# A 96-row gather, a fold split over two engines, a shuffle in pieces and earlier loads in the start of a Fourier and feed-forward kernel

## The chip, the cores and the metric

The kernel runs on one core of a Trainium2 chip. The metric is the device time of one execution in microseconds (us). Every execution quoted here counts as fast: none took over 1.5% more than the fastest of the same kernel. Engines are named as the profile names them: PE is TensorE's matmuls and PEld its weight loads, DVE is VectorE, ACT is ScalarE, POOL is GpSimd, and SP is SyncE, which here only issues transfers. A `q` after an engine's name (SPq, POOLq) means its sequencer.

## The reference, cut to what matters

The input is 8 batches of 3008 rows by 256 columns. The kernel takes the real part of a two-dimensional Fourier transform of each batch and sends all rows through a gated feed-forward block.

```python
def _attn_ref(x):                       # x: (8, 3008, 256)
    X = np.fft.fft(x, axis=1)
    X = np.fft.fft(X, axis=2)
    return X.real.astype(np.float32)

def _moe_ref(x, w_gate, w_val, w_out):  # x: (24064, 256), d_ff = 1536
    gate = np.maximum(x @ w_gate, 0.0)
    val = x @ w_val
    return (gate * val @ w_out).astype(np.float32)
```

## The kernel before

The kernel writes the 3008 rows as 94 times 32. For one batch the work is a chain:

1. `load_x`: half of x comes by two plain transfers (`xl`), the other half, in reversed order of blocks, by a gather (`xh`): a transfer that fetches one row per index, with one index for each partition (row of the on-chip memory).
2. `fold`: sums and differences of mirrored rows and columns, elementwise, into `eo`.
3. `stage1`: 17 row groups of `eo` times small Fourier tables on TensorE, into `t1`.
4. `shuffle`: `t1` is written to memory (`Td`) and read back in another order (`t4`).
5. `rotate` and `stage2`: the second half of the transform along the rows, into `pq`.
6. The main loop: 288 steps (`plus`, `minus`, `out_piece`), 36 per batch. The transform along the columns is multiplied into the weights beforehand (the weight products `psw`, into `wc`, `ws`, `wm`).

Batch 0 does 1 to 5 before the loop. Batch b+1 does 3 to 5 inside the loop of batch b, at step numbers set in the table `extra`. The parts that matter here, with cuts marked by `...`:

```python
NA, NB = 94, 32
def load_x(b):
    xl = xp.tile([NA, J, D], F32, tag="xl")
    xh = xp.tile([NA, NB // 2, D], F32, tag="xh")
    for p0, n in ((0, 80), (80, 14)):
        nc.sync.dma_start(out=xl[p0:p0 + n], in_=...)
    nc.gpsimd.indirect_dma_start(out=xh[:]..., in_=...,
                                 in_offset=bass.IndirectOffsetOnAxis(ap=ix[:, b:b + 1], axis=0))
...
def shuffle(b):
    nc.sync.dma_start(out=Td[b], in_=t1t.pop(b)[:]...)
    t4 = tp.tile([128, NKA, D], BF16, tag="t4")
    nc.sync.dma_start(out=t4[:], in_=view(Td[b], 0, [[D, 128], [128 * D, NKA], [1, D]]))
...
ix = const.tile([NA, B], I32, tag="ix")
nc.gpsimd.iota(ix[:], pattern=[[2 * NA, B]], base=2 * NA - 1, channel_multiplier=-2)
load_x(0)
...                                   # weight loads, w_out, all tables on VectorE
fold(0, nc.vector)
for c in range(8):
    stage1(0, c, "act" if c % 2 else "dve")
shuffle(0)
load_x(1)
fold(1, nc.gpsimd)
for i in range(2):                    # weight products
    for n in range(DF // 512):
        ...
rotate(0)
...                                   # stage2(0), then the main loop with
for b in range(B):
    t0 = b * NBLK * NF
    # load_x(b+2) at t0+10, fold(b+2) on GpSimd at t0+11,
    # stage1(b+1) at t0+1..8, shuffle at t0+9, rotate at t0+16, stage2 at t0+18+3i
```

Of the kernel before, what the change touches and what calls it, by code (L numbers as in the profile page):

```python
# [10 lines left out]
F32 = mybir.dt.float32  # L11
# [20 lines left out]
def sin_of(nc, sp, out, t, n, shape):  # L32

    q = sp.tile(shape, F32, tag="q")
    nc.vector.tensor_scalar(q[:], t, scalar1=1.0 / n, scalar2=RND, op0=ALU.mult, op1=ALU.add)
    nc.vector.tensor_scalar(q[:], q[:], scalar1=-RND, scalar2=float(n), op0=ALU.add, op1=ALU.mult)
    nc.vector.tensor_tensor(q[:], t, q[:], op=ALU.subtract)
    nc.scalar.activation(out, q[:], ACTF.Sin, scale=2.0 * math.pi / n * (1.0 - 2e-7))
# [3 lines left out]
def kernel(ctx: ExitStack, tc, x, w_gate, w_val, w_out, out):  # L42
# [9 lines left out]
    NKA = 12  # L52
# [16 lines left out]
    def load_x(b):  # L69
        xl = xp.tile([NA, J, D], F32, tag="xl")  # L70
        xh = xp.tile([NA, NB // 2, D], F32, tag="xh")
        for p0, n in ((0, 80), (80, 14)):
            nc.sync.dma_start(out=xl[p0:p0 + n],  # L73
                              in_=view(x, b * S * D + p0 * NB * D, [[NB * D, n], [1, J * D]]))
# [4 lines left out]
        xt[b] = (xl, xh)  # L79

    eot = {}

    def fold(b, eng):
        xl, xh = xt.pop(b)
        xc = xp.tile([NA, J - 2, D], F32, tag="xc")
        eo = tp.tile([NA, J, D], BF16, tag="eo")
        n = J - 2
        rev = free(xh[:], n * D, [-D, n], [1, D])
        eng.tensor_tensor(xc[:], xl[:, 1:J - 1, :], rev, op=ALU.subtract)  # L89
        eng.tensor_tensor(xl[:, 1:J - 1, :], xl[:, 1:J - 1, :], rev, op=ALU.add)  # L90
        eng.tensor_tensor(eo[:, :, 1:H], xl[:, :, 1:H], free(xl[:], D - 1, [D, J], [-1, H - 1]), op=ALU.add)
        eng.tensor_tensor(eo[:, 1:J - 1, H + 1:D], xc[:, :, 1:H],
                          free(xc[:], D - 1, [D, n], [-1, H - 1]), op=ALU.subtract)
        eng.tensor_tensor(free(eo[:], H + 1, [(J - 1) * D, 2], [1, H - 1]),
                          free(xl[:], 1, [(J - 1) * D, 2], [1, H - 1]),
                          free(xl[:], D - 1, [(J - 1) * D, 2], [-1, H - 1]), op=ALU.subtract)
        eng.tensor_copy(free(eo[:], 0, [D, J], [H, 2]), free(xl[:], 0, [D, J], [H, 2]))  # L97
        eot[b] = eo
# [3 lines left out]
    def stage1(b, c, evac):  # L102
        if c == 0:
            t1t[b] = tp.tile([96, 16, D], BF16, tag="t1", bufs=1, name="t1")
        t1, eo = t1t[b], eot[b]
# [20 lines left out]
    def shuffle(b):  # L126
        nc.sync.dma_start(out=Td[b], in_=t1t.pop(b)[:].rearrange("p j d -> p (j d)"))
        t4 = tp.tile([128, NKA, D], BF16, tag="t4")
        nc.sync.dma_start(out=t4[:], in_=view(Td[b], 0, [[D, 128], [128 * D, NKA], [1, D]]))
        t4t[b] = t4  # L130
# [23 lines left out]
    ix = const.tile([NA, B], I32, tag="ix")  # L154
    nc.gpsimd.iota(ix[:], pattern=[[2 * NA, B]], base=2 * NA - 1, channel_multiplier=-2)
    load_x(0)
# [11 lines left out]
    with tc.tile_pool(name="st", bufs=1, space=SB) as st, \  # L168
# [8 lines left out]
        nc.gpsimd.dma_start(out=wo[:], in_=view(w_out, 0, [[D, 128], [128 * D, NF], [1, D]]))  # L177
# [12 lines left out]
        for off in (S // 4, S // 2):  # L190
# [3 lines left out]
            sin_of(nc, sp, tb[:], t2[:], S, [NA, J, 48])  # L194
# [6 lines left out]
        nc.vector.memset(w1[:, 0, :], 0.0)  # L201

# [14 lines left out]
        nc.vector.tensor_scalar(z[:], jj[:], scalar1=0.0, scalar2=None, op0=ALU.is_equal)  # L217
        zs = sp.tile([128, 1], F32, tag="zs")
        nc.vector.tensor_tensor(zs[:], z[:], sl[:], op=ALU.mult)
        mul = sp.tile([128, 1], F32, tag="mul")  # L220
        nc.vector.tensor_scalar(mul[:], zs[:], scalar1=16.0, scalar2=None, op0=ALU.mult)
        nc.vector.tensor_tensor(mul[:], mul[:], jj[:], op=ALU.add)
        offs = []

        for cs, (o0, d1) in enumerate(((8.0, -8.0), (16.0, -8.0))):
            o = sp.tile([128, 1], F32, tag=f"off{cs}")
            nc.vector.tensor_scalar(o[:], sl[:], scalar1=d1, scalar2=o0 - 8.0, op0=ALU.mult, op1=ALU.add)
# [212 lines left out]
```

## Time and profile before

| Reading | Value |
|---|---|
| time, median of the runs beside the change | 821.86 us |
| span of the profiled run | 820.7 us |
| first gather issued, and landed | 1.79 us, 51.9 us |
| main loop starts | 108.6 us |
| TensorE waits inside the loop | 24.4 us and 9.5 us, both in batch 0 |
| TensorE busy from 200 to 280 us | 79.88 of 80 us |

From 200 us on TensorE is full. What can be won lies before. The view of waits lists who waited for whom, for how many us in total, how often, and the longest. These are TensorE's four longest in the kernel before:

```profile
PE ps_240 L115 <- DVE eo L97: 65.3, 1, 65.3
PE ps_434 L115 <- POOL eo L97: 24.4, 1, 24.4
PE psr L135 <- DMA t_276<-Td: 12.7, 1, 12.7
PE psr L135 <- DMA t_590<-Td: 9.5, 1, 9.5
```

The first is batch 0's fold on VectorE, the second batch 1's fold on GpSimd inside the loop. The last two are the reads of the two batches' shuffles. The timeline gives, for each instruction, its start, its duration, engine, source line, operation and shapes, and in brackets how long the engine was idle before it and what ended that:

```profile
51.93 4.15 DVE L89 TENSOR_TENSOR xc<-xl,xh 94x3840 f32<-94x3840 f32 x1 [27.54 <-DMA xh<-in_x_dram,ix]
...
104.95 0.19 PE L135 MATMUL psr<-t_276,rot 128*128 128x12 bf16 x1 [12.69 <-DMA t_276<-Td]
...
108.58 0.63 PE L325 MATMUL G<-pq,wc_84 128*128 128x512 bf16 x1
...
110.22 8.27 POOL L89 TENSOR_TENSOR xc<-xl,xh 94x3840 f32<-94x3840 f32 x1 [46.09 <-DMA xl<-in_x_dram]
```

VectorE stood idle for 27.54 us until the gather had landed. The view of windows shows why the gather took so long. After the length of the window it gives the busy us (and the instructions) of PE, PEld, DVE, ACT and POOL, then TensorE's granted clock. Its last two columns are the mean busy share of the 16 DMA engines, and the GB/s that they moved:

```profile
30.00:35.00 5.00, 0.00 (x0) 0.00 (x0) 0.00 (x0) 0.00 (x0) 0.00 (x0) 1.00 0.12 52
...
40.00:45.00 5.00, 0.00 (x0) 0.00 (x0) 0.00 (x0) 0.00 (x0) 0.00 (x0) 1.00 0.13 53
...
200.00:280.00 80.00, 79.88 (x533) 50.91 (x532) 55.29 (x84) 47.79 (x83) 26.60 (x8) 1.00 0.36 99
```

Between 30 and 45 us no engine runs an instruction, and the gather, together with what is left of other loads, keeps a share of 0.12 to 0.13 busy: two engines' worth of 16. The summary of this gather's eight executions says that this is not only so at the start:

```profile
DMA to landing us min/median/max: 34.8/37.5/50.1
```

### The profile page before, as it was taken

To read this page: it belongs to the slowest core of one execution; us is meant where nothing else is said; L and a number is where in the kernel's file an instruction comes from. 1 tells how busy PE (TensorE), PEld (TensorE's weight loads), DVE (VectorE), ACT (ScalarE), POOL (GpSimd) and SP (SyncE) were. 2 spreads that over 40 slices of the span, in tenths; PEclk is the share of its full clock that TensorE was granted. 3 is DMA by queue.
4 is the path that set the end of the run, shared out by engine and by line. 5 is a ranking of instruction groups with operands and counts; after the bars stand their busy time and mean duration, and the time that the engine had idled before them with its cause. 6 is when DMAs were issued, how large, how long until landed. Compare 5 with 4: busy or idle time off the path is not lost.

```text
span 820.7 us, 12157 instructions
## 1 busy us (share of the span) xinstructions
PE 696.3 (85%) x4432; PEld 433.2 (53%) x4432; DVE 491.5 (60%) x767; ACT 406.4 (50%) x699; POOL 203.8 (25%) x66
## 2 busy tenths in 40 slices
PE   0007433859999999999999999999999999999997
PEld 0004211336666666666666666666666666666655
DVE  6143121636776676667666766676666666666662
ACT  1002211525565656565656565656565655655552
POOL 2001067009300930094009400850093000000000
PEclk9999865979999999999999999999999999999999
DMA  9302510262137213621271226212711141111112
GB/s 242 77 28 79 130 23 10 88 135 51 53 99 184 50 54 98 168 67 48 88 193 47 61 89 177 64 50 81 192 55 43 26 127 27 51 29 48 35 43 76
DMA packets 31852, 67.37 MB, mean 82 GB/s; under 512 B 9040, under 2 KB 22864, under 8 KB 29520
## 3 DMA queue, kind: packets, MB, share of 16 engines
q1 hardware_dynamic: 24096, 53.48, 25.8%
q0 software_dynamic: 7696, 13.13, 4.9%
q8 instruction: 34, 0.56, 0.3%
q14 instruction: 26, 0.21, 0.1%
HBM read 36.42 MB, written 30.93 MB: 82 GB/s over the span
## 4 chain that ended last, share of the span: by engine, by line
PE 74%; DVE 7%; DMA 6%; POOL 4%; another core or an unknown queue 3%; SPq 2%; ACT 2%; issue 1%; POOLq 0%; DVEq 0%
PE po L359 28%; PE V L336 9%; PE G L325 7%; PE G L326 7%; PE V L326 7%; PE V L325 7%; PE G L336 7%; DVE h L329 2%; DMA t_590<-Td 2%; SPq L73 2%; DMA xl<-in_x_dram 2%; ACT gs L339 1%; DMA Td<-t_433 1%; DMA Td<-t_239 1%
## 5 line engine op out<-in xcount | busy, mean ns | idle before, releaser
L341 DVE TENSOR_TENSOR h<-gs,V 128x512 bf16<-128x512 f32 x288 | 198.1, 688 | 199.9 <-ACT gs L339 147.4
L359 PE MATMUL po<-wo,h 128*128 128x256 bf16 x2304 | 297.8, 273 | 0.0
L339 ACT ACTIVATE gs<-G 128x512 f32<-128x512 f32 x288 | 172.2, 598 | 241.4 <-PE G L336 241.4
L359 PEld LDWEIGHTS <-h 128*128 128x128 bf16 x2304 | 223.4, 98 | 74.3 <-issue 10.5
L329 DVE TENSOR_TENSOR h<-gs,V 128x512 bf16<-128x512 f32 x288 | 197.8, 687 | 10.9 <-ACT gs L328 5.7
L328 ACT ACTIVATE gs<-G 128x512 f32<-128x512 f32 x288 | 172.3, 598 | 30.2 <-PE G L326 13.6
L89 POOL TENSOR_TENSOR xc<-xl,xh 94x3840 f32<-94x3840 f32 x7 | 58.2, 8314 | 362.8 <-DMA xl<-in_x_dram 362.8
L336 PE MATMUL V<-pq,wm_89 128*128 128x512 bf16 x288 | 109.0, 379 | 5.0 <-DVE h L329 3.6
L336 PE MATMUL G<-pq,wm_88 128*128 128x512 bf16 x288 | 109.8, 381 | 1.0 <-ACT gs L328 0.8
L326 PE MATMUL V<-pq,ws_87 128*128 128x512 bf16 x288 | 109.8, 381 | 0.0
L325 PE MATMUL V<-pq,wc_85 128*128 128x512 bf16 x288 | 109.7, 381 | 0.0
L326 PE MATMUL G<-pq,ws_86 128*128 128x512 bf16 x288 | 109.6, 381 | 0.0
L325 PE MATMUL G<-pq,wc_84 128*128 128x512 bf16 x288 | 109.5, 380 | 0.0
L90 POOL TENSOR_TENSOR xl<-xl,xh 94x3840 f32<-94x3840 f32 x7 | 58.2, 8316 | 0.6
L115 PE MATMUL ps_240<-eo,wz 94*96 94x129 bf16 (+1 forms) x4 | 0.6, 303 | 65.3 <-DVE eo L97 65.3
L325 PEld LDWEIGHTS <-wc_84 128*128 128x128 bf16 x288 | 27.8, 97 | 52.8 <-issue 42.0
L115 PEld LDWEIGHTS <-wz 94*96 94x96 bf16 x32 | 3.2, 136 | 91.2 <-issue 77.3
L365 ACT COPY os<-po 128x512 f32<-128x512 f32 x48 | 28.1, 585 | 43.8 <-PE po L359 43.8
L326 PEld LDWEIGHTS <-ws_87 128*128 128x128 bf16 x288 | 28.2, 98 | 34.7 <-issue 0.8
L325 PEld LDWEIGHTS <-wc_85 128*128 128x128 bf16 x288 | 28.0, 97 | 34.8 <-issue 0.8
L326 PEld LDWEIGHTS <-ws_86 128*128 128x128 bf16 x288 | 27.8, 97 | 34.5 <-issue 0.6
L363 DVE COPY os<-po 128x512 f32<-128x512 f32 x48 | 33.2, 692 | 8.4 <-PE po L359 8.4
(341 smaller groups left out, 381.7 us busy)
## 6 DMA issues: line engine op xcount, KB each, us to landing
out_dram<-os SPq DMA_DIRECT2D x176, 128.0 KB, 2.6
xl<-in_x_dram SPq DMA_DIRECT2D x8, 1360.0 KB, 11.8
xl<-in_x_dram SPq DMA_DIRECT2D x8, 238.0 KB
wst_100<-in_moe_w_gate_dram SPq DMA_DIRECT2D x2, 768.0 KB, 23.9
wst_103<-in_moe_w_val_dram SPq DMA_DIRECT2D x2, 768.0 KB, 34.5
out_dram<-os SPq DMA_DIRECT2D x16, 96.0 KB, 1.8
wo<-in_moe_w_out_dram POOLq DMA_DIRECT2D x1, 768.0 KB, 52.3
Td<-t_239 SPq DMA_DIRECT2D x1, 768.0 KB, 9.3
```

The lines of the kernel that those rows point to most:

```text
L89: eng.tensor_tensor(xc[:], xl[:, 1:J - 1, :], rev, op=ALU.subtract)
L90: eng.tensor_tensor(xl[:, 1:J - 1, :], xl[:, 1:J - 1, :], rev, op=ALU.add)
L325: nc.tensor.matmul(acc[:], lhsT=wc[i][:, fs], rhs=pq[:, 0, :], start=True, stop=False)
L326: nc.tensor.matmul(acc[:], lhsT=ws[i][:, fs], rhs=pq[:, 1, :], start=False, stop=True)
L328: nc.scalar.activation(gs[:], G[:], ACTF.Relu)
L329: nc.vector.tensor_tensor(h[:, 0, :], gs[:], V[:], op=ALU.mult)
L336: nc.tensor.matmul(acc[:], lhsT=wm[i][:, fs], rhs=pq[:, 1, :], start=False, stop=True, skip_group_check=True)
L339: nc.scalar.activation(gs[:], G[:], ACTF.Relu)
L341: nc.vector.tensor_tensor(free(h[:], 512 + NB - 1, [NB, 16], [-1, NB]), gs[:].rearrange("p (a k) -> p a k", k=NB), V[:].rearrange("p (a k) ...
L359: nc.tensor.matmul(po[:, s % 2, :], lhsT=ht[b, blk, ff][:, sg, g * 128:(g + 1) * 128], rhs=wo[:, ff, :], start=(ff == 0), stop=(ff == NF - 1))
L363: nc.vector.tensor_copy(os_[:, s - 1:s + 1, :], po[:])
L365: nc.scalar.copy(os_[:, s - 1:s + 1, :], po[:])
```

## The change

The intent is to shorten the start. Its parts are:

- the gather uses 96 rows instead of 94; the two extra indices are clamped to 0 and their rows are not used;
- batch 0's fold is split by rows: rows 1 to 11 and the ends on VectorE, rows 12 to 15 on GpSimd;
- most of the small tables move from VectorE to GpSimd, which computes them before its rows;
- batch 0's shuffle is written in four pieces and read in three;
- batch 1's loads, and w_out, are issued before the shuffle's read instead of after it (and w_out instead of at the very start);
- in the loop of batch 0, batch 1's stages come at later steps; those of the other batches shift by a few;
- smaller things: stage 1 takes row group 0 last and is emptied mostly by ScalarE, and the groups of weight products come in another order.

The diff, cut to its core:

```diff
-        xh = xp.tile([NA, NB // 2, D], F32, tag="xh")
+        xh = xp.tile([96, NB // 2, D], F32, tag="xh")
...
-    ix = const.tile([NA, B], I32, tag="ix")
+    ix = const.tile([96, B], I32, tag="ix")
     nc.gpsimd.iota(ix[:], pattern=[[2 * NA, B]], base=2 * NA - 1, channel_multiplier=-2)
-    load_x(0)
+    nc.gpsimd.tensor_scalar(ix[:], ix[:], scalar1=0, scalar2=None, op0=ALU.max)
+    load_x(0, nc.sync)
...
-        nc.gpsimd.dma_start(out=wo[:], in_=view(w_out, 0, ...))
...
+        pl = nc.gpsimd          # the small tables now on pl, their sines still on ScalarE
...
-        fold(0, nc.vector)
-        for c in range(8):
-            stage1(0, c, "act" if c % 2 else "dve")
-        shuffle(0)
-        load_x(1)
-        fold(1, nc.gpsimd)
+        fold(0, nc.vector, 2, 8)
+        fold(0, nc.vector, 8, 12)
+        fold(0, nc.gpsimd, 12, 16)
+        fold_ends(0, nc.vector)
+        fold(0, nc.vector, 1, 2)
+        for k, c in enumerate((1, 2, 3, 4, 5, 6, 7, 0)):
+            stage1(0, c, "dve" if k in (5, 7) else "act")
+        for k in (2, 4, 6, 0):
+            shuffle_out(0, k, k + 2)
+        load_x(1, nc.scalar)
+        nc.gpsimd.dma_start(out=wo[:], in_=view(w_out, 0, ...))
+        for blk in range(NBLK):
+            shuffle_in(0, 4 * blk, 4 * blk + 4)
+        fold_all(1)
...
+        tl, t1, tr, t2, d2 = (17, 16, 28, 29, 1) if b == 0 else (10, 4, 19, 20, 2)
+        # load_x(b+2) at tl, stage1(b+1) from t1, shuffle at t1+8, rotate at tr, stage2 from t2 every d2
```

More of the change, by code (lines that the diff above doesn't have):

```diff
@@ L29, in free, with sin_of @@
     return bass.AP(ap.tensor, ap.offset + offset, [part] + [list(d) for d in dims])
-def sin_of(nc, sp, out, t, n, shape):
+def sin_of(nc, eng, sp, out, t, n, shape):
     q = sp.tile(shape, F32, tag="q")
-    nc.vector.tensor_scalar(q[:], t, scalar1=1.0 / n, scalar2=RND, op0=ALU.mult, op1=ALU.add)
-    nc.vector.tensor_scalar(q[:], q[:], scalar1=-RND, scalar2=float(n), op0=ALU.add, op1=ALU.mult)
-    nc.vector.tensor_tensor(q[:], t, q[:], op=ALU.subtract)
+    eng.tensor_scalar(q[:], t, scalar1=1.0 / n, scalar2=RND, op0=ALU.mult, op1=ALU.add)
+    eng.tensor_scalar(q[:], q[:], scalar1=-RND, scalar2=float(n), op0=ALU.add, op1=ALU.mult)
+    eng.tensor_tensor(q[:], t, q[:], op=ALU.subtract)
     nc.scalar.activation(out, q[:], ACTF.Sin, scale=2.0 * math.pi / n * (1.0 - 2e-7))
@@ L67, with load_x @@
     xt = {}
-    def load_x(b):
+    def load_x(b, q):
         xl = xp.tile([NA, J, D], F32, tag="xl")
-        xh = xp.tile([NA, NB // 2, D], F32, tag="xh")
+        xh = xp.tile([96, NB // 2, D], F32, tag="xh")
         for p0, n in ((0, 80), (80, 14)):
-            nc.sync.dma_start(out=xl[p0:p0 + n],
-                              in_=view(x, b * S * D + p0 * NB * D, [[NB * D, n], [1, J * D]]))
+            q.dma_start(out=xl[p0:p0 + n],
+                        in_=view(x, b * S * D + p0 * NB * D, [[NB * D, n], [1, J * D]]))
         nc.gpsimd.indirect_dma_start(out=xh[:].rearrange("p j d -> p (j d)"), out_offset=None,
@@ L78, in load_x @@
                                      in_offset=bass.IndirectOffsetOnAxis(ap=ix[:, b:b + 1], axis=0))
-        xt[b] = (xl, xh)
-    eot = {}
-    def fold(b, eng):
-        xl, xh = xt.pop(b)
-        xc = xp.tile([NA, J - 2, D], F32, tag="xc")
-        eo = tp.tile([NA, J, D], BF16, tag="eo")
-        n = J - 2
-        rev = free(xh[:], n * D, [-D, n], [1, D])
-        eng.tensor_tensor(xc[:], xl[:, 1:J - 1, :], rev, op=ALU.subtract)
-        eng.tensor_tensor(xl[:, 1:J - 1, :], xl[:, 1:J - 1, :], rev, op=ALU.add)
-        eng.tensor_tensor(eo[:, :, 1:H], xl[:, :, 1:H], free(xl[:], D - 1, [D, J], [-1, H - 1]), op=ALU.add)
-        eng.tensor_tensor(eo[:, 1:J - 1, H + 1:D], xc[:, :, 1:H],
-                          free(xc[:], D - 1, [D, n], [-1, H - 1]), op=ALU.subtract)
-        eng.tensor_tensor(free(eo[:], H + 1, [(J - 1) * D, 2], [1, H - 1]),
-                          free(xl[:], 1, [(J - 1) * D, 2], [1, H - 1]),
-                          free(xl[:], D - 1, [(J - 1) * D, 2], [-1, H - 1]), op=ALU.subtract)
-        eng.tensor_copy(free(eo[:], 0, [D, J], [H, 2]), free(xl[:], 0, [D, J], [H, 2]))
-        eot[b] = eo
+        xt[b] = (xl, xh, xp.tile([NA, J - 2, D], F32, tag="xc", name="xc"),
+                 tp.tile([NA, J, D], BF16, tag="eo", name="eo"))
@@ new lines, in fold @@
+    def fold(b, eng, lo, hi):
+        xl, xh, xc, eo = xt[b]
+        n = hi - lo
+        x1, c1, e1 = xl[:, lo:hi, :], xc[:, lo - 1:hi - 1, :], eo[:, lo:hi, :]
+        rev = free(xh[0:NA], (NB // 2 - lo) * D, [-D, n], [1, D])
+        eng.tensor_tensor(c1, x1, rev, op=ALU.subtract)
+        eng.tensor_tensor(x1, x1, rev, op=ALU.add)
+        eng.tensor_tensor(e1[:, :, 1:H], x1[:, :, 1:H], free(x1, D - 1, [D, n], [-1, H - 1]), op=ALU.add)
+        eng.tensor_tensor(e1[:, :, H + 1:D], c1[:, :, 1:H], free(c1, D - 1, [D, n], [-1, H - 1]), op=ALU.subtract)
+        eng.tensor_copy(free(e1, 0, [D, n], [H, 2]), free(x1, 0, [D, n], [H, 2]))
@@ new lines, in fold_ends, with fold_all @@
+    def fold_ends(b, eng):
+        xl, xh, xc, eo = xt[b]
+        for op, o in ((ALU.add, 1), (ALU.subtract, H + 1)):
+            eng.tensor_tensor(free(eo[:], o, [(J - 1) * D, 2], [1, H - 1]),
+                              free(xl[:], 1, [(J - 1) * D, 2], [1, H - 1]),
+                              free(xl[:], D - 1, [(J - 1) * D, 2], [-1, H - 1]), op=op)
+        eng.tensor_copy(free(eo[:], 0, [(J - 1) * D, 2], [H, 2]), free(xl[:], 0, [(J - 1) * D, 2], [H, 2]))
+    def fold_all(b):
+        fold(b, nc.gpsimd, 1, J - 1)
+        fold_ends(b, nc.gpsimd)
@@ L100 @@
     t1t = {}
     def stage1(b, c, evac):
-        if c == 0:
+        if b not in t1t:
             t1t[b] = tp.tile([96, 16, D], BF16, tag="t1", bufs=1, name="t1")
-        t1, eo = t1t[b], eot[b]
+        t1, eo = t1t[b], xt[b][3]
         ps = psd.tile([128, 512], F32, tag="d", name="ps1")
@@ L124, with shuffle_out, shuffle_in @@
     t4t = {}
-    def shuffle(b):
-        nc.sync.dma_start(out=Td[b], in_=t1t.pop(b)[:].rearrange("p j d -> p (j d)"))
-        t4 = tp.tile([128, NKA, D], BF16, tag="t4")
-        nc.sync.dma_start(out=t4[:], in_=view(Td[b], 0, [[D, 128], [128 * D, NKA], [1, D]]))
-        t4t[b] = t4
+    def shuffle_out(b, c0, c1):
+        nc.sync.dma_start(out=view(Td[b], 2 * c0 * D, [[16 * D, 96], [1, 2 * (c1 - c0) * D]]),
+                          in_=t1t[b][:, 2 * c0:2 * c1, :].rearrange("p j d -> p (j d)"))
+    def shuffle_in(b, a0, a1):
+        if b not in t4t:
+            t4t[b] = tp.tile([128, NKA, D], BF16, tag="t4", name="t4")
+        nc.sync.dma_start(out=t4t[b][:, a0:a1, :],
+                          in_=view(Td[b], a0 * 128 * D, [[D, 128], [128 * D, a1 - a0], [1, D]]))
     def rotate(b):
@@ L176 @@
             wst.append(t)
-        nc.gpsimd.dma_start(out=wo[:], in_=view(w_out, 0, [[D, 128], [128 * D, NF], [1, D]]))
         si = sp.tile([NA, J], F32, tag="si")
@@ L193 @@
             tb = sp.tile([NA, J, 48], BF16, tag="tb")
-            sin_of(nc, sp, tb[:], t2[:], S, [NA, J, 48])
+            sin_of(nc, nc.vector, sp, tb[:], t2[:], S, [NA, J, 48])
             tab.append(tb)
@@ L201 @@
         nc.vector.memset(w1[:, 0, :], 0.0)
-        pi = sp.tile([128, 1], I32, tag="pi")
-        nc.gpsimd.iota(pi[:], pattern=[[0, 1]], base=0, channel_multiplier=1)
-        def bits(shift, mask):
-            ti = sp.tile([128, 1], I32, tag=f"b{shift}{mask}i")
-            nc.vector.tensor_scalar(ti[:], pi[:], scalar1=shift, scalar2=mask,
-                                    op0=ALU.logical_shift_right, op1=ALU.bitwise_and)
-            tf = sp.tile([128, 1], F32, tag=f"b{shift}{mask}f")
-            nc.vector.tensor_copy(tf[:], ti[:])
-            return tf
@@ L215 @@
-        jj, sl, up = bits(0, 15), bits(4, 1), bits(5, 3)
-        z = sp.tile([128, 1], F32, tag="z")
-        nc.vector.tensor_scalar(z[:], jj[:], scalar1=0.0, scalar2=None, op0=ALU.is_equal)
-        zs = sp.tile([128, 1], F32, tag="zs")
-        nc.vector.tensor_tensor(zs[:], z[:], sl[:], op=ALU.mult)
-        mul = sp.tile([128, 1], F32, tag="mul")
-        nc.vector.tensor_scalar(mul[:], zs[:], scalar1=16.0, scalar2=None, op0=ALU.mult)
-        nc.vector.tensor_tensor(mul[:], mul[:], jj[:], op=ALU.add)
@@ L223 @@
-        offs = []
-        for cs, (o0, d1) in enumerate(((8.0, -8.0), (16.0, -8.0))):
-            o = sp.tile([128, 1], F32, tag=f"off{cs}")
-            nc.vector.tensor_scalar(o[:], sl[:], scalar1=d1, scalar2=o0 - 8.0, op0=ALU.mult, op1=ALU.add)
-            nz = sp.tile([128, 1], F32, tag="nz")
-            nc.vector.tensor_scalar(nz[:], z[:], scalar1=-1.0, scalar2=1.0, op0=ALU.mult, op1=ALU.add)
-            nc.vector.tensor_tensor(o[:], o[:], nz[:], op=ALU.mult)
-            nc.vector.tensor_scalar(o[:], o[:], scalar1=8.0, scalar2=None, op0=ALU.add)
-            offs.append(o)
@@ L233 @@
-        kbi = sp.tile([128, 4, NB], F32, tag="kbi")
-        nc.gpsimd.iota(kbi[:], pattern=[[0, 4], [1, NB]], base=0, channel_multiplier=0,
-                       allow_small_or_imprecise_dtypes=True)
-        ui = sp.tile([128, 4, NB], F32, tag="ui")
-        nc.gpsimd.iota(ui[:], pattern=[[1, 4], [0, NB]], base=0, channel_multiplier=0,
-                       allow_small_or_imprecise_dtypes=True)
-        nc.vector.tensor_scalar(ui[:], ui[:], scalar1=up[:], scalar2=None, op0=ALU.is_equal)
-        for cs in range(2):
-            t2 = sp.tile([128, 4, NB], F32, tag="m2t")
-            nc.vector.tensor_scalar(t2[:], kbi[:], scalar1=mul[:], scalar2=offs[cs][:],
-                                    op0=ALU.mult, op1=ALU.add)
-            sv = sp.tile([128, 4, NB], F32, tag="m2s")
-            sin_of(nc, sp, sv[:], t2[:], NB, [128, 4, NB])
-            nc.vector.tensor_tensor(m2[:, cs, :].rearrange("p (u k) -> p u k", u=4), sv[:], ui[:], op=ALU.mult)
@@ L249 @@
-        di = sp.tile([128, 4, 2, 16], F32, tag="di")
-        nc.gpsimd.iota(di[:], pattern=[[-32, 4], [-16, 2], [-1, 16]], base=0, channel_multiplier=1,
-                       allow_small_or_imprecise_dtypes=True)
-        ro = sp.tile([128, 4, 2, 16], F32, tag="ro")
-        nc.vector.memset(ro[:], 0.0)
-        nc.vector.tensor_scalar(ro[:, :, 0, 1:16], di[:, :, 0, 1:16], scalar1=16.0, scalar2=-1.0,
-                                op0=ALU.is_equal, op1=ALU.mult)
-        nc.vector.tensor_scalar(ro[:, :, 1, 1:16], di[:, :, 1, 1:16], scalar1=-16.0, scalar2=None, op0=ALU.is_equal)
@@ L257 @@
-        nc.vector.tensor_scalar(ro[:, :, :, 0], di[:, :, :, 0], scalar1=0.0, scalar2=None, op0=ALU.is_equal)
-        nc.vector.tensor_copy(rot[:], ro[:].rearrange("p u s j -> p (u s j)"))
-        pf = sp.tile([128, 1], F32, tag="pf")
-        nc.vector.tensor_copy(pf[:], pi[:])
-        nc.vector.tensor_scalar(s2[:], pf[:], scalar1=1.0, scalar2=-2.0, op0=ALU.min, op1=ALU.mult)
         cd = st.tile([128, 2, 2, H], F32, tag="cd")
@@ L277 @@
             nc.vector.tensor_scalar(dd[:, 1, 0:1], dd[:, 1, 0:1], scalar1=float(D // 4), scalar2=None, op0=ALU.add)
-            sin_of(nc, sp, cd[:, c, :, :], dd[:], D, [128, 2, H])
-        fold(0, nc.vector)
-        for c in range(8):
-            stage1(0, c, "act" if c % 2 else "dve")
-        shuffle(0)
-        load_x(1)
-        fold(1, nc.gpsimd)
-        for i in range(2):
-            for n in range(DF // 512):
+            sin_of(nc, nc.vector, sp, cd[:, c, :, :], dd[:], D, [128, 2, H])
@@ new lines, with bits @@
+        pl = nc.gpsimd
+        pi = sp.tile([128, 1], I32, tag="pi")
+        nc.gpsimd.iota(pi[:], pattern=[[0, 1]], base=0, channel_multiplier=1)
+        def bits(shift, mask):
+            ti = sp.tile([128, 1], I32, tag=f"b{shift}{mask}i")
+            nc.vector.tensor_scalar(ti[:], pi[:], scalar1=shift, scalar2=mask,
+                                    op0=ALU.logical_shift_right, op1=ALU.bitwise_and)
+            tf = sp.tile([128, 1], F32, tag=f"b{shift}{mask}f")
+            nc.vector.tensor_copy(tf[:], ti[:])
+            return tf
@@ new lines @@
+        jj, sl, up = bits(0, 15), bits(4, 1), bits(5, 3)
+        z = sp.tile([128, 1], F32, tag="z")
+        pl.tensor_scalar(z[:], jj[:], scalar1=0.0, scalar2=None, op0=ALU.is_equal)
+        zs = sp.tile([128, 1], F32, tag="zs")
+        pl.tensor_tensor(zs[:], z[:], sl[:], op=ALU.mult)
+        mul = sp.tile([128, 1], F32, tag="mul")
+        pl.tensor_scalar(mul[:], zs[:], scalar1=16.0, scalar2=None, op0=ALU.mult)
+        pl.tensor_tensor(mul[:], mul[:], jj[:], op=ALU.add)
+        offs = []
@@ new lines @@
+        for cs, (o0, d1) in enumerate(((8.0, -8.0), (16.0, -8.0))):
+            o = sp.tile([128, 1], F32, tag=f"off{cs}")
+            pl.tensor_scalar(o[:], sl[:], scalar1=d1, scalar2=o0 - 8.0, op0=ALU.mult, op1=ALU.add)
+            nz = sp.tile([128, 1], F32, tag="nz")
+            pl.tensor_scalar(nz[:], z[:], scalar1=-1.0, scalar2=1.0, op0=ALU.mult, op1=ALU.add)
+            pl.tensor_tensor(o[:], o[:], nz[:], op=ALU.mult)
+            pl.tensor_scalar(o[:], o[:], scalar1=8.0, scalar2=None, op0=ALU.add)
+            offs.append(o)
@@ new lines @@
+        kbi = sp.tile([128, 4, NB], F32, tag="kbi")
+        nc.gpsimd.iota(kbi[:], pattern=[[0, 4], [1, NB]], base=0, channel_multiplier=0,
+                       allow_small_or_imprecise_dtypes=True)
+        ui = sp.tile([128, 4, NB], F32, tag="ui")
+        nc.gpsimd.iota(ui[:], pattern=[[1, 4], [0, NB]], base=0, channel_multiplier=0,
+                       allow_small_or_imprecise_dtypes=True)
+        pl.tensor_scalar(ui[:], ui[:], scalar1=up[:], scalar2=None, op0=ALU.is_equal)
+        for cs in range(2):
+            t2 = sp.tile([128, 4, NB], F32, tag="m2t")
+            pl.tensor_scalar(t2[:], kbi[:], scalar1=mul[:], scalar2=offs[cs][:],
+                                    op0=ALU.mult, op1=ALU.add)
+            sv = sp.tile([128, 4, NB], F32, tag="m2s")
+            sin_of(nc, pl, sp, sv[:], t2[:], NB, [128, 4, NB])
+            pl.tensor_tensor(m2[:, cs, :].rearrange("p (u k) -> p u k", u=4), sv[:], ui[:], op=ALU.mult)
@@ new lines @@
+        di = sp.tile([128, 4, 2, 16], F32, tag="di")
+        nc.gpsimd.iota(di[:], pattern=[[-32, 4], [-16, 2], [-1, 16]], base=0, channel_multiplier=1,
+                       allow_small_or_imprecise_dtypes=True)
+        ro = sp.tile([128, 4, 2, 16], F32, tag="ro")
+        pl.memset(ro[:], 0.0)
+        pl.tensor_scalar(ro[:, :, 0, 1:16], di[:, :, 0, 1:16], scalar1=16.0, scalar2=-1.0,
+                                op0=ALU.is_equal, op1=ALU.mult)
+        pl.tensor_scalar(ro[:, :, 1, 1:16], di[:, :, 1, 1:16], scalar1=-16.0, scalar2=None, op0=ALU.is_equal)
@@ new lines @@
+        pl.tensor_scalar(ro[:, :, :, 0], di[:, :, :, 0], scalar1=0.0, scalar2=None, op0=ALU.is_equal)
+        pl.tensor_copy(rot[:], ro[:].rearrange("p u s j -> p (u s j)"))
+        pf = sp.tile([128, 1], F32, tag="pf")
+        pl.tensor_copy(pf[:], pi[:])
+        pl.tensor_scalar(s2[:], pf[:], scalar1=1.0, scalar2=-2.0, op0=ALU.min, op1=ALU.mult)
+        fold(0, nc.vector, 2, 8)
[3 more added lines that the diff above has]
+        fold(0, nc.vector, 1, 2)
@@ L289 @@
+        for k, c in enumerate((1, 2, 3, 4, 5, 6, 7, 0)):
[3 more added lines that the diff above has]
+        load_x(1, nc.scalar)
+        nc.gpsimd.dma_start(out=wo[:], in_=view(w_out, 0, [[D, 128], [128 * D, NF], [1, D]]))
+        for blk in range(NBLK):
+            shuffle_in(0, 4 * blk, 4 * blk + 4)
+        fold_all(1)
+        for n in range(DF // 512):
+            for i in range(2):
                 for cs in range(2):
@@ L383, with at @@
     extra = {}
+    def at(t, fn, *args):
+        extra.setdefault(t, []).append(lambda: fn(*args))
     for b in range(B):
         t0 = b * NBLK * NF
+        tl, t1, tr, t2, d2 = (17, 16, 28, 29, 1) if b == 0 else (10, 4, 19, 20, 2)
         if b + 2 < B:
-            extra.setdefault(t0 + 10, []).append(lambda b=b: load_x(b + 2))
-            extra.setdefault(t0 + 11, []).append(lambda b=b: fold(b + 2, nc.gpsimd))
+            at(t0 + tl, load_x, b + 2, nc.sync)
+            at(t0 + tl + 1, fold_all, b + 2)
         if b + 1 < B:
             for c in range(8):
-                extra.setdefault(t0 + 1 + c, []).append(
-                    lambda b=b, c=c: stage1(b + 1, c, "act" if c % 2 else "dve"))
-            extra.setdefault(t0 + 9, []).append(lambda b=b: shuffle(b + 1))
-            extra.setdefault(t0 + 16, []).append(lambda b=b: rotate(b + 1))
+                at(t0 + t1 + c, stage1, b + 1, c, "act" if c % 2 else "dve")
+            at(t0 + t1 + 8, shuffle_out, b + 1, 0, 8)
+            at(t0 + t1 + 8, shuffle_in, b + 1, 0, NKA)
+            at(t0 + tr, rotate, b + 1)
             for i in range(6):
-                extra.setdefault(t0 + 18 + 3 * i, []).append(
-                    lambda b=b, i=i: stage2(b + 1, i // 2, i % 2, "dve" if i % 2 else "act"))
+                at(t0 + t2 + d2 * i, stage2, b + 1, i // 2, i % 2, "dve" if i % 2 else "act")
     n = len(steps)
```

## The prediction

> What bounds it now. The slice table and the windows show two regimes. From 200 us on, TensorE is 99.8% busy (79.88 of 80 us) at full clock; the change removes no matmuls, so that part stays. Before it TensorE waits. The chain of waits and the timeline: VectorE waits 27.5 us for the gather of x (issued 1.79, landed 51.9); fold of batch 0 on VectorE 51.9 to 65.3; stage 1 to 71.3; Td written in 9.3 us; its read and batch 1's loads contend, and rotate starts at 104.9; main loop from 108.6. In the loop TensorE waits from 112.4 to 136.8 for batch 1's fold on GpSimd, and from 170.9 to 180.6 for batch 1's shuffle, with slow matmuls (0.43 us apart instead of 0.22) after each wait.
>
> Why the gather is slow: while it runs alone (25 to 52 us) the DMA share is 0.13, two of 16 engines, at 45 to 60 GB/s. [...] So 96 rows should use 16 engines, and free the two that held up wo, weights and shuffle.
>
> After, estimates from these durations:
> - x and weights, 6.3 MB at about 310 GB/s (the 10 to 20 us windows): gather landed about 20 us. VectorE's tables end about 18 us (24.4 less the moved 7).
> - 11 of 15 inner rows plus ends on VectorE: about 11 us. GpSimd first does some 30 small table operations (about 10 us, from 18 us), then 4 rows at 2.15 ns per element, 7 us. [...] I put GpSimd's end, the fold's last, at 40 us, range 35 to 47.
> - Stage 1 to 42 us. Weight products (48 x 0.43 = 20.6 us) to 63 us; the shuffle, beside loads and wo (4.7 MB), lands about 57 us, hidden under them. Rotate and stage 2: 3.8 us. Main loop starts about 67 us instead of 108.6: gain 42 us.
> - Batch 1's fold runs about 58 to 85 us, before its stage 1 (now step 16, about 103 us): the 24.4 us wait goes.
> - Its shuffle has four steps (8.7 us) against about 10 us needed: the 9.7 us wait shrinks to 0 to 2. Slow restarts (about 4 us) go too.
> - Given back: batch 1's stage 1 (8 x 0.43 = 3.5 us) moves from the first 12 steps, which take 2.21 us with or without it, into steps where TensorE is full.
>
> Sum: 822 - 42 - 24.4 - 8.5 - 4 + 3.5 = 747 us. All of it is on the critical path, since TensorE idles there. Range 734 to 762. Faster by over 2%: 0.98; within 2%: 0.015; slower: 0.005.
>
> What would show it: gather landing near 20 us with DMA share near 1; GpSimd's fold of rows 12 to 16 ending last, VectorE and GpSimd operations lengthened while both run; the main loop near 67 us, preceded by weight products and not by a DMA wait; no wait for GpSimd at batch 1's stage 1; at most 2 us at its rotate; the part after 200 us as busy as before.
>
> What would make it wrong: the gather still on few engines; GpSimd blocked much longer by VectorE (stage 1 ending after 47 us); the shuffle starved by batch 1's loads, so that rotate waits past 63 us; a load issued from ScalarE's queue blocking its evictions; the order of fold's pieces tying VectorE to GpSimd.

The second was the reason for 5 of the 40 us at GpSimd's end: the steps that stand come to 35 us (18 + 10 + 7), and the other 5 us were the author's guess at what VectorE and GpSimd lose by running together. The sum comes to 747 us (746.6), but the loop's start at 67 us, and so the gain of 42 us, includes that guess.

## The result, and the profile after

The changed kernel takes 752.02 us (median of 4 runs, 751.76 to 754.34), against 821.86 us. The ratio is 0.9156, with a 95% interval of 0.9136 to 0.9176. Ratios in this document are the mean time of one kernel's fast runs over the mean time of the fast runs of the kernel before in the same rounds, so not quite the ratio of the medians quoted. The span of the profiled run is 750.4 us. The prediction was 747 us, 734 to 762.

TensorE's waits after, from the same view:

```profile
PE ps_257 L117 <- DVE eo L92: 26.8, 1, 26.8
PE ps_277 L117 <- POOL eo L92: 8.5, 1, 8.5
...
PE psr L146 <- DMA t_969<-Td: 1.6, 1, 1.6
...
PE psr L146 <- DMA t_304<-Td: 0.4, 1, 0.4
```

TensorE's first wait now ends 38.5 us earlier, but it is only for the fold's first rows: the whole fold of batch 0 ends at 42.0 us instead of 65.3, 23.3 us earlier. The wait for batch 1's fold is gone: the one wait for GpSimd that is left is for batch 0's own rows. The two waits for shuffles are down from 12.7 and 9.5 us to 0.4 and 1.6 us. The windows after, the first one while the first gather still ran, and the gather's landing times:

```profile
15.00:20.00 5.00, 0.00 (x0) 0.00 (x0) 0.99 (x7) 0.42 (x1) 3.31 (x15) 1.00 0.95 223
...
200.00:280.00 80.00, 79.83 (x533) 50.85 (x532) 55.12 (x84) 47.35 (x82) 25.24 (x9) 1.00 0.37 95
```

```profile
DMA to landing us min/median/max: 9.6/11.0/19.0
```

The DMA engines are nearly all busy (a share of 0.95) while the gather and the weight loads run, and the median gather takes 11.0 us instead of 37.5. From 200 us on nothing changed. The timeline of the new start:

```profile
20.76 1.89 DVE L88 TENSOR_TENSOR xc<-xl,xh 94x1536 f32<-94x1536 f32 x1 [4.67 <-DMA xh<-in_x_dram,ix]
...
34.53 2.34 POOL L88 TENSOR_TENSOR xc<-xl,xh 94x1024 f32<-94x1024 f32 x1
...
42.06 0.59 PE L117 MATMUL ps_277<-eo,w_82 94*96 94x256 bf16 x2 [8.48 <-POOL eo L92]
...
44.34 5.78 PE L313 MATMUL psw<-wst_103,cd 128*128 128x512 f32 x8
49.95 3.60 PE L313 MATMUL psw<-wst_106,cd 128*128 128x512 f32 x8
...
67.67 0.18 PE L146 MATMUL psr<-t_304,rot 128*128 128x12 bf16 x1 [0.39 <-DMA t_304<-Td]
...
70.87 0.38 PE L346 MATMUL G<-pq,wc_87 128*128 128x512 bf16 x1
```

VectorE folds from 20.76 us, when the gather lands. GpSimd gets to its rows only at 34.53, after VectorE has finished its own at 33.3, so the two halves of the split do not overlap at all, and TensorE waits 8.48 us for GpSimd's. The weight products then run from 44.34 to about 67.3 us, and the main loop starts at 70.87 us, 37.7 us earlier than before (108.58 - 70.87).

The saving adds up as follows. The loop starts 37.7 us earlier, the wait for batch 1's fold gives 24.4 us, and the shuffle of batch 1 gives 7.9 us (9.5 - 1.6). The sum is 70.0 us, and the spans differ by 70.3 us (820.7 - 750.4). What is left, quicker restarts of TensorE against stage 1 of batch 1 in fuller steps, about cancels; these two were not measured apart. The slow restarts are in the trace of the kernel before: right after the waits that ended at 104.9, 136.8 and 180.6 us the granted clock read 0.50, and in the loop the matmuls of 512 columns came 0.43 us apart instead of 0.22. The changed kernel's loop starts with 0.22 us, at a clock of 1.00 (68 to 71 us).

Why does GpSimd come so late? The timeline of the same kernel shows pairs of the same table operation, one started before VectorE's fold (20.76 us) and one beside it:

```profile
20.21 0.46 POOL L270 TENSOR_SCALAR t_204<-kbi,mul,o 128x128 f32<-128x128 f32 x1
20.75 0.30 POOL L35 TENSOR_SCALAR q<-t_204 128x128 f32<-128x128 f32 x1
...
25.87 2.19 POOL L270 TENSOR_SCALAR t_213<-kbi,mul,o 128x128 f32<-128x128 f32 x1
28.14 1.17 POOL L35 TENSOR_SCALAR q<-t_213 128x128 f32<-128x128 f32 x1
```

Beside VectorE's fold the two operations took 2.19 and 1.17 us instead of 0.46 and 0.30. So GpSimd is held up while VectorE folds; what holds it up, the trace does not show. In e2 and e10 below, where the gather landed after GpSimd's tables were done, the same tables took 12.3 us; here they took 18.9, from 15.7 to 34.6 us. GpSimd's issuing of a gather is longer beside VectorE's fold too: the instruction for batch 1's gather took 3.53 us there in the kernel before and 3.02 us in e1, against 1.65 and 1.11 us for the first gather of the same kernels, with VectorE idle.

### The profile page after: what moved, and what is told of

The parts are those of the page before. It is cut to its first block, busy times and chain, and to the rows that moved or that the text cites. A ratio compares the mean times of both kernels' runs of the same rounds, so it can differ in the third digit from the quotient of the medians.

```text
span 750.4 us, 12199 instructions
## 1 busy us (share of the span) xinstructions
PE 692.4 (92%) x4432; PEld 430.6 (57%) x4432; DVE 481.0 (64%) x747; ACT 408.3 (54%) x701; POOL 221.6 (30%) x116
## 4 chain that ended last, share of the span: by engine, by line
PE 82%; DVE 6%; ACT 4%; POOL 3%; issue 3%; DMA 1%; ACTq 0%; POOLq 0%; DVEq 0%
PE po L380 30%; PE V L357 10%; PE G L347 7%; PE G L346 7%; PE V L347 7%; PE V L346 7%; PE G L357 7%; DVE h L350 4%; PE psw L313 3%; ACT gs L360 2%; ACT gs L349 1%; DVE h L362 1%; DMA t_969<-Td 1%; DMA Td<-t_719 1%; DVE q L37 0%
## 5 line engine op out<-in xcount | busy, mean ns | idle before, releaser
L88 POOL TENSOR_TENSOR xc<-xl,xh 94x3840 f32<-94x3840 f32 (+1 forms) x8 | 60.6, 7574 | 302.2 <-DMA xl<-in_x_dram 268.8
L89 POOL TENSOR_TENSOR xl<-xl,xh 94x3840 f32<-94x3840 f32 (+1 forms) x8 | 60.6, 7578 | 0.6
L346 PEld LDWEIGHTS <-wc_87 128*128 128x128 bf16 x288 | 27.7, 96 | 54.5 <-issue 43.2
L347 PEld LDWEIGHTS <-ws_90 128*128 128x128 bf16 x288 | 28.0, 97 | 34.2
L346 PEld LDWEIGHTS <-wc_88 128*128 128x128 bf16 x288 | 27.8, 97 | 34.3
L347 PEld LDWEIGHTS <-ws_89 128*128 128x128 bf16 x288 | 27.7, 96 | 34.2
L117 PEld LDWEIGHTS <-w_82 94*96 94x96 bf16 x120 | 15.7, 131 | 50.5 <-issue 28.1
L357 PEld LDWEIGHTS <-wm_92 128*128 128x128 bf16 x288 | 28.2, 98 | 9.6 <-issue 6.5
```

Source lines behind the costliest of these rows:

```text
L88: eng.tensor_tensor(c1, x1, rev, op=ALU.subtract)
L89: eng.tensor_tensor(x1, x1, rev, op=ALU.add)
L346: nc.tensor.matmul(acc[:], lhsT=wc[i][:, fs], rhs=pq[:, 0, :], start=True, stop=False)
L347: nc.tensor.matmul(acc[:], lhsT=ws[i][:, fs], rhs=pq[:, 1, :], start=False, stop=True)
L357: nc.tensor.matmul(acc[:], lhsT=wm[i][:, fs], rhs=pq[:, 1, :], start=False, stop=True, skip_group_check=True)
```

## The experiments

Two theories of the gain were set against each other first. Theory G: the two-engine gather caused most of the loss, also through what it did to other transfers. Rival S: the rearrangement of the start makes the gain. Then came the question of what bounds the new start, and whether each of the change's other parts pays. All kernels below gave correct results.

| Run | Base and edit | Median us | Ratio to before (95%) |
|---|---|---|---|
| after | the change | 752.02 | 0.9156 (0.9136 to 0.9176) |
| e1_gather_only | before, gather on 96 rows | 761.21 | 0.9260 (0.9244 to 0.9275) |
| e2_gather94 | after, gather on 94 rows | 814.36 | 0.9911 (0.9893 to 0.9929) |
| e10_gather95 | after, gather on 95 rows | 768.35 | 0.9338 (0.9324 to 0.9353) |
| e3_fold_vector | after, fold not split | 745.81 | 0.9102 (0.9047 to 0.9158) |
| e5_tables_vector | after, tables on VectorE | 755.49 | 0.9193 (0.9151 to 0.9235) |
| e4_old_loop | after, old step numbers | 762.25 | 0.9269 (0.9254 to 0.9285) |
| e11_shuffle_whole | after, shuffle in one piece | 751.65 | 0.9137 (0.9123 to 0.9151) |
| e6_loads_late | e3, loads behind the shuffle | 743.68 | 0.9033 (0.9020 to 0.9045) |
| e7_weights_early | e3, weight products early | 760.05 | 0.9238 (0.9224 to 0.9252) |
| e8_both | e3, both | 743.48 | 0.9010 (0.8986 to 0.9033) |
| e9_both_later_steps | e8, batch 1 three steps later | 734.59 | 0.8924 (0.8912 to 0.8936) |

### e1_gather_only: the gather alone

```diff
-        xh = xp.tile([NA, NB // 2, D], F32, tag="xh")
+        xh = xp.tile([96, NB // 2, D], F32, tag="xh")
...
-        rev = free(xh[:], n * D, [-D, n], [1, D])
+        rev = free(xh[0:NA], n * D, [-D, n], [1, D])
...
-    ix = const.tile([NA, B], I32, tag="ix")
+    ix = const.tile([96, B], I32, tag="ix")
...
+    nc.gpsimd.tensor_scalar(ix[:], ix[:], scalar1=0, scalar2=None, op0=ALU.max)
```

> The kernel before with nothing changed but the gather on 96 rows. Theory G (the two-engine gather is the cause of most of the loss, also of what it does to other transfers): it lands at about 22 us instead of 51.9, VectorE folds from 24.4 (its tables) to 38, the main loop starts at about 68 us, TensorE then waits about 12 us for GpSimd's fold of batch 1 and not at all for its shuffle: 755 us, nearly all of the whole change's gain. Rival S (the split fold, the pieces and the new order of steps make the gain, the gather only the first wait): the gain stops at the 27.5 us of VectorE's wait, 794 us.

It measured 761.21 us. Two rows more in the gather win 61 of the change's 70 us, so rival S fails. The loop starts at about 68 us, even before the whole change's 70.87. The one large wait left in the loop is that for batch 1's fold:

```profile
PE ps L115 <- POOL eo L97: 15.7, 1, 15.7
```

The waits say where the 61 us come from: TensorE's first wait is 28.2 us shorter (65.3 to 37.1), both waits for shuffles (12.7 and 9.5 us) are gone, and the wait for batch 1's fold is 8.7 us shorter, 59.1 us in all. So about half of what the slow gather cost came through what it held up.

I had expected 12 us in the wait for batch 1's fold and no more loss. That wait is 3.7 us longer, which leaves about 2.5 of the 6 us by which I missed without an account.

### e2_gather94: everything but the gather

```diff
-        xh = xp.tile([96, NB // 2, D], F32, tag="xh")
+        xh = xp.tile([NA, NB // 2, D], F32, tag="xh")
-    ix = const.tile([96, B], I32, tag="ix")
+    ix = const.tile([NA, B], I32, tag="ix")
```

> The changed kernel with the gather put back on 94 rows. Theory G: first gather lands at 40 to 45 us, main loop starts near 90 us, gathers of batches 1 and 2 hold up the shuffles on two engines again (TensorE waits some 15 us at batch 1's rotate): about 784 us. Rival S: the schedule hides the slow gathers, at most 20 us lost: 772 us or less.

It measured 814.36 us. The rest of the change is worth less than 1% without the gather. I undersized the damage by 30 us: the first gather landed at 51.2 us, not 40 to 45, and the shuffle suffered far more. TensorE's waits for the shuffles in this run:

```profile
PE psr L146 <- DMA t<-Td: 33.9, 3, 27.2
```

Batch 0's write now took 19.45 us and its read 27.54 us in the chain of waits. Batch 1's gather, its plain loads and w_out were issued between 68.5 and 70.2 us, just before the last piece of the write (71.4). The slow gather alone does not explain this: in the kernel before it was ahead of the shuffle too (issued at 60.6, the write at 71.3), but the plain loads came behind the read, and the write took 9.3 us and the read 24.3. So loading early, w_out included, seems to cost about 13 us beside a slow gather, while beside the quick one e6 below puts its cost at 2 us. No run with the slow gather and late loads was made, so this is argued, not shown.

### e10_gather95: the rule behind the number

```diff
-        xh = xp.tile([96, NB // 2, D], F32, tag="xh")
+        xh = xp.tile([95, NB // 2, D], F32, tag="xh")
-    ix = const.tile([96, B], I32, tag="ix")
+    ix = const.tile([95, B], I32, tag="ix")
```

> The changed kernel with a gather of 95 rows instead of 96, which tells the divisor rule from mere padding. Divisor rule (95 has 5 as its largest divisor up to 16): five engines, first gather landed between the 20.7 us of 96 rows and the 51.2 us of 94, at about 30 us; time 762 to 780 us. Rival (any even spread, or 94 was a special case): 752 us, as with 96. Rival (odd row counts fall to one engine): 814 us or more.

It measured 768.35 us, in the expected range, with the first gather landed at 32.5 us. While the gather and a rest of other loads ran, the window reads:

```profile
25.00:30.00 5.00, 0.00 (x0) 0.00 (x0) 0.00 (x0) 0.24 (x1) 2.57 (x9) 1.00 0.32 133
```

A share of 0.32 is five engines of 16 (0.3125), and 133 GB/s is 2.5 times the 53 GB/s of two. The divisor rule of the expectation, taken with the number of gathered rows, 94, 95 or 96, gives 2, 5 and 16 engines. The traces fit all three: shares of 0.12 to 0.13, of 0.32, and, for 96 rows, of 1.04 in a stretch of the changed kernel where batch 3's gather ran alone (the share of a window can read a little above 1):

```profile
138.00:141.00 3.00, 3.00 (x26) 2.14 (x24) 1.40 (x3) 1.78 (x3) 0.00 (x0) 1.00 1.04 238
```

The time of 768 us lies clear of the 752 of 96 rows, so padding as such is not what helps. The number of gathered rows decides here: the source view in the code has 1504 rows in all three kernels. No other count was run, so the rule is shown for these three alone.

### e3_fold_vector: the split undone

```diff
-        fold(0, nc.gpsimd, 12, 16)
+        fold(0, nc.vector, 12, 16)
```

> The changed kernel with rows 12 to 16 of batch 0's fold on VectorE too (no split). Theory P (GpSimd ends the fold late, at 42.0, because its tables are stretched by VectorE's operations): VectorE ends the whole fold at about 37 us, so the weight products start 5 us sooner: 747 us. Rival (the split earns its place): VectorE alone ends after 42 us, and the time is 752 us or more.

It measured 745.81 us, with runs of 745.09, 746.54, 754.15 and 744.66. Its interval overlaps that of the change because of the one run at 754, which I can't explain (a hint follows under e7); the traces tell the two apart. VectorE alone finished the whole fold at 36.2 us, 5.8 us before GpSimd ended in the changed kernel (42.0), and the weight products began at 36.64 us instead of 44.34. In the profiled pair the split costs time, because GpSimd comes to its rows late. That is not the whole reason. In e10 GpSimd's tables were done before the gather landed, and both engines began their rows at once:

```profile
32.48 1.75 DVE L88 TENSOR_TENSOR xc<-xl,xh 94x1536 f32<-94x1536 f32 x1 [16.09 <-DMA xh<-in_x_dram,ix]
32.53 3.90 POOL L88 TENSOR_TENSOR xc<-xl,xh 94x1024 f32<-94x1024 f32 x1 [4.28 <-DMA xh<-in_x_dram,ix]
34.27 3.77 DVE L89 TENSOR_TENSOR xl<-xl,xh 94x1536 f32<-94x1536 f32 x1
36.51 3.73 POOL L89 TENSOR_TENSOR xl<-xl,xh 94x1024 f32<-94x1024 f32 x1
```

VectorE's second operation took 3.77 us instead of the 1.75 of e5, where it ran alone, and GpSimd's took 3.90 and 3.73 instead of 2.33. The whole fold took 17.5 us (32.5 to 50.0); VectorE alone in e3 took 16.6 (19.7 to 36.2). So the split gains nothing here even when GpSimd is on time.

### e5_tables_vector: the move of the tables undone

```diff
-        pl = nc.gpsimd
+        pl = nc.vector
```

> The changed kernel with the small tables computed on VectorE again, the split fold kept. Theory P (GpSimd's tables, stretched by VectorE's folds, are what delays GpSimd's rows to 42.0 us): GpSimd folds its rows from 20.8 to 28 or 31 us, VectorE starts 2 us later and ends at about 35, weight products start at 37 instead of 44: 745 us. Rival (moving the tables off VectorE helps): VectorE's 7 us more show in the start, 752 us or more.

It measured 750.61, 751.58, 759.4 and 759.52 us: two levels, 9 us apart. I don't know what chooses the level (a hint follows under e7). Neither side's expectation is met cleanly. The profiled run, at the lower level, shows where my 745 us went wrong. GpSimd did fold early, from 19.84 to 27.1 us. But VectorE's operations were held up in turn:

```profile
17.92 0.34 DVE L270 TENSOR_SCALAR t<-kbi,mul,o 128x128 f32<-128x128 f32 x1
...
19.77 2.48 DVE L270 TENSOR_SCALAR t<-kbi,mul,o 128x128 f32<-128x128 f32 x1
19.84 2.33 POOL L88 TENSOR_TENSOR xc<-xl,xh 94x1024 f32<-94x1024 f32 x1 [14.74 <-DMA xh<-in_x_dram,ix]
22.25 2.33 POOL L89 TENSOR_TENSOR xl<-xl,xh 94x1024 f32<-94x1024 f32 x1
22.29 2.38 DVE L35 TENSOR_SCALAR q<-t 128x128 f32<-128x128 f32 x1
```

The same VectorE operation that took 0.34 us alone took 2.48 us beside GpSimd's first row operation, and the next one as long as GpSimd's second. VectorE's fold began at 29.04 us instead of the 23 that I had expected, and ended at 40.4. In both runs the engine that had the short operations was held up beside the other's long ones.

### e4_old_loop: the old step numbers

```diff
-        tl, t1, tr, t2, d2 = (17, 16, 28, 29, 1) if b == 0 else (10, 4, 19, 20, 2)
+        tl, t1, tr, t2, d2 = 10, 1, 16, 18, 3
```

> The changed kernel with the step numbers of the kernel before (stage 1 of batch 1 at step 1, rotate at 16). Theory: TensorE waits about 14 us at step 1 for GpSimd's fold of batch 1 (ends at 88 us), wins back 3.5 us of stage 1 hidden in the first steps and 1.6 us at the rotate: 761 us. Rival (batch 1's loads come so early that the step numbers no longer matter): 752 us within 2.

It measured 762.25 us, within 1.3 us of the expectation, and the expected wait is in the profile:

```profile
PE ps L121 <- POOL eo L100: 13.6, 1, 13.6
```

So the new step numbers are worth 10 us. The edit puts back those of all batches, but the wait of 13.6 us is batch 1's. They are the part of the change that pays beside the gather: e1, which lacks them, has a like wait of 15.7 us.

### e11_shuffle_whole: the pieces undone

```diff
-        for k in (2, 4, 6, 0):
-            shuffle_out(0, k, k + 2)
+        shuffle_out(0, 0, 8)
...
-        for blk in range(NBLK):
-            shuffle_in(0, 4 * blk, 4 * blk + 4)
+        shuffle_in(0, 0, NKA)
```

> The changed kernel with batch 0's shuffle in one write and one read instead of four and three pieces. Theory: the whole write is then issued at 45 us, after batch 1's loads, and lands behind them, some 4 us later than the last piece did; the read follows, rotate at 72 instead of 67.7 us: 757 us. Rival (the pieces bring nothing, the last piece sets the end either way): 752 us within 2.

It measured 751.65 us against 752.02, so the rival holds: the pieces bring nothing here. The whole write was issued at 45.4 us, the time of the last piece in the changed kernel, and the read followed at 61.7 us, where that of the pieces was issued at 61.6. The last piece set the end either way.

### e6, e7 and e8: two chains that end together

In the changed kernel the shuffle landed 0.4 us after the weight products had ended, near 67.3 us. I had expected it to land 6 us before them. So the start of the loop hangs on two chains of nearly equal length, and shortening one alone should win nothing. The three kernels build on e3. The first puts batch 1's loads and w_out behind the shuffle's read (a GpSimd copy of three elements of `t4` holds the gather back):

```diff
-        load_x(1, nc.scalar)
-        nc.gpsimd.dma_start(out=wo[:], ...)
         for blk in range(NBLK):
             shuffle_in(0, 4 * blk, 4 * blk + 4)
+        seen = sp.tile([128, NBLK], F32, tag="seen")
+        nc.gpsimd.tensor_copy(seen[:], free(t4t[0][:], 0, [4 * D, NBLK]))
+        load_x(1, nc.sync)
+        nc.gpsimd.dma_start(out=wo[:], ...)
```

> The kernel of e3_fold_vector with batch 1's loads and w_out behind the read of batch 0's shuffle instead of beside it. Theory T (two chains of nearly equal length start the main loop: stage 1 then weight products on TensorE, and the shuffle starved by batch 1's loads): the shuffle lands at about 50 us instead of 61, but the weight products still end at 60, so only the 1.8 us wait at the rotate goes: 744 us. Rival D (the loads beside the shuffle are what starts the loop late): main loop 8 us or more earlier, 738 us or less.

The second moves four of six groups of weight products between the groups of stage 1. ScalarE empties them, `s2` is computed first, and the sines of the stage 2 table come after stage 1. The last point also removes a wait: in the changed kernel ScalarE stood 5.80 us before such a sine, waiting for GpSimd's table, while it had stage 1's first groups to empty, and TensorE waited 3.9 us for that. Of the diff only the main added lines are shown:

```diff
+        weights(0, 0, True)
+        weights(0, 1, True)
+        for c in (1, 2, 3):
+            stage1(0, c, "act")
+        weights(1, 0, True)
+        weights(1, 1, True)
+        for c in (4, 5):
+            stage1(0, c, "act")
+        for k, c in enumerate((6, 7, 0)):
+            stage1(0, c, "act" if k == 1 else "dve")
...
         fold_all(1)
+        weights(2, 0, False)
+        weights(2, 1, False)
```

> The kernel of e3_fold_vector with four of the six groups of weight products moved between the stage 1 groups, where TensorE waits. Theory T: the shuffle still lands at 61 us or later, so the time stays at 745 to 748 us. Rival W (the weight products alone set the start): main loop 8 us or more earlier, 738 us or less.

The third has both edits:

> The kernel of e3_fold_vector with both: loads behind the shuffle and four groups of weight products early. Theory T: only both together move the start, main loop at about 54 us instead of 64, 736 us, 8 us or more better than the better of the two alone. Rivals D or W: no better than that one alone.

e6 measured 743.68 us, as theory T said: the shuffle was no longer starved, and yet the loop started only 1 us earlier, since the weight products still ended at 59.2 us (59.9 in e3). How long the transfers of batch 0's shuffle took to land (both directions, minimum, median and maximum), in the changed kernel:

```profile
DMA to landing us min/median/max: 2.1/4.7/16.2
```

and in e6:

```profile
DMA to landing us min/median/max: 2.1/2.9/3.3
```

The longest was a piece of the write: 16.2 us beside batch 1's loads (17.0 in e3, on which e6 builds), and 3.3 us at most without them. That was a write of 192 KB beside about 4 MB of loads. The loads were issued from ScalarE and GpSimd, the write from SyncE, and the write was slowed all the same, while the DMA share read 1.03 to 1.04 (45 to 60 us).

e7 measured 760.05 us. The direction was as theory T said, no gain, but it lost 14 us, which I had not sized. Its shuffle waits show where:

```profile
PE psr L146 <- DMA t<-Td: 23.6, 2, 15.9
```

Stage 1 ended 5 us later than in e3, behind the weight products, its last pieces again met batch 1's loads, and TensorE waited 15.9 us at batch 0's rotate. The other 7.7 us are at batch 1's rotate, where e3 waited 1.8. No run tests why that second wait grew, but the two traces differ in an order. In e3 the read of batch 1's shuffle was issued just before batch 3's gather, which GpSimd issues once it has folded batch 2:

```profile
125.55 0.38 SPq L140 DMA_DIRECT2D t<-Td  x1
125.81 0.94 POOL L76 DMA_INDIRECT xh<-in_x_dram,ix  x1
```

In e7 the gather came first:

```profile
131.20 0.94 POOL L76 DMA_INDIRECT xh<-in_x_dram,ix  x1
132.56 0.38 SPq L140 DMA_DIRECT2D t<-Td  x1
```

The read landed in 5.4 us in e3 and in 11.0 us in e7. This may also be what the slow runs of e3 and e5 have in common: in e3's profiled run the read was ahead by 0.26 us and in e5's by 0.68, and in the slow runs the mean granted clock was lower (0.989 in e3; 0.993 and 0.991 in e5; 0.996 to 0.999 in the others), as it is in e4 (0.988), whose loop has a long wait. The slow runs left no trace, so this is a guess.

e8 measured 743.48 us where 736 was expected (two of its five runs took 739.22 and 740.40). Its loop did start at 55.1 us, 9 us earlier than that of e3, but the gain did not reach the end:

```profile
PE ps L121 <- POOL eo L100: 4.4, 1, 4.4
PE psr L146 <- DMA t<-Td: 2.3, 1, 2.3
```

With batch 1's loads behind the shuffle, its fold on GpSimd ended at 96 us, and an earlier loop reached batch 1's stage 1 before that. After that wait the granted clock read 0.50 from 96 to 100 us, and the loop's matmuls came 0.43 us apart instead of 0.22. A new wait had taken the place of the old one.

### e9_both_later_steps

```diff
-        tl, t1, tr, t2, d2 = (17, 16, 28, 29, 1) if b == 0 else (10, 4, 19, 20, 2)
+        tl, t1, tr, t2, d2 = (20, 19, 32, 33, 1) if b == 0 else (10, 4, 19, 20, 2)
```

> The kernel of e8_both with batch 1's stage 1 at step 19 instead of 16, its rotate at 32 instead of 28. Theory: e8's loop began 9 us earlier but TensorE then waited 4.4 us for GpSimd's fold of batch 1, restarted slowly (about 2 us) and waited 2.3 us at the rotate; with three steps more all of it goes: 736 us. Rival (the gain is lost for another reason): 742 us or more.

It measured 734.59 us (733.73 to 734.92), a ratio of 0.8924 to the kernel before. It is faster than both kernels of this case: 17 us faster than the changed one by the medians. Neither wait of e8 is left; the one wait for a shuffle is 0.6 us. That two chains end together fits all four kernels: late loads alone won 2 us, early products alone lost 14, both together with the step numbers fitted won 11 (745.81 - 734.59). Theory T's figures for e7 and e8 missed, because it did not foresee the waits in the loop. Later steps without early products were not run; the wait that they could have removed from e6 is 1.6 us.

## Why the prediction was right

| Step of the prediction | Expected | Measured |
|---|---|---|
| first gather landed | 20 us | 20.7 us |
| VectorE's tables end | 18 us | 16.1 us |
| GpSimd ends the fold | 40 us (35 to 47) | 42.0 us |
| weight products end | 63 us | 67.3 us |
| batch 0's shuffle landed | 57 us | 67.7 us |
| main loop starts | 67 us | 70.9 us |
| wait for batch 1's fold in the loop | 0 | 0 |
| wait at batch 1's rotate | 0 to 2 us | 1.6 us |
| time | 747 us | 752.0 us |

- **The gather.** That 94 rows use two engines was read from the share of 0.13. That 96 would use 16 no trace of the kernel before showed; the changed kernel does, with a share of 1.04. e1 and e2 show that this is the cause of most of the gain, and e10, with a share of 0.32, that the divisor rule fits a third row count.
- **GpSimd ends the fold last, and contention with VectorE is why.** This came as predicted, 2 us later than the 40 us given, 5 us of which were a guess at the contention: GpSimd's tables took 18.9 us beside VectorE's fold, and 12.3 us where they were done before it. e3 shows that the split does not pay, and e10 that it would not pay with GpSimd on time either.
- **Batch 1's fold moves off the critical path.** This is confirmed by the wait that vanished and by e4, which brings back 13.6 us of it.
- **The start of the loop** was 3.9 us late. That is nearly all of the 5 us by which the sum missed. The mis-sized term is "Stage 1 to 42 us. Weight products (48 x 0.43 = 20.6 us) to 63 us": stage 1 ended 2.3 us late, nearly all of it GpSimd's 2 us, and the 48 matmuls took 23 us, the first eight of them 5.78 us instead of 3.60. That resembles the slow matmuls after waits in the kernel before (0.43 us apart instead of 0.22, at a granted clock of 0.50), but here the granted clock read 1.00 (42 to 50 us), and no run tests it: in e3, where the last long wait was 5.5 us, the 48 took 23.3.
- **The shuffle** was the weakest step. "Lands about 57 us, hidden under them" was 10 us too early: the written pieces took up to 16.2 us beside batch 1's loads. That it cost only 0.4 us is luck, as the weight products ended at nearly the same time, themselves 4 us late. The prediction named this risk ("starved by batch 1's loads, so that rotate waits past 63 us"), and e6 shows that the loads are the cause.
- **The three last waits of the sum** (24.4, 8.5 and 4 us less 3.5 given back) held: 24.4 and 7.9 us were measured, and the rest about cancels.

What stays open: what chooses between e5's two levels, and e3's single slow run; the 2.5 us of e1's miss; and whether the order of gather and read is the cause of batch 1's longer wait in e7. The prediction did not see that the split, the pieces and the early loads would not pay. It priced the change as a whole.

## What to carry to other kernels

Look at the DMA share while one transfer runs alone: if the share is a small fraction of 16 engines, try another row count (here 94, 95 and 96 rows gave shares of 0.13, 0.32 and 1.04); here two unused rows were worth more than a rearranged schedule. When a start has several chains, find out which end together before shortening one, and after each gain ask which wait comes next: here late loads, early weight products and later steps paid only as a set. Splitting the fold between VectorE and GpSimd was no gain here, because each was held up beside the other: in e10 VectorE's second operation took 3.77 us instead of 1.75, and GpSimd's first two took 3.90 and 3.73 us instead of 2.33.
